# xLSTM attention before two mixture-of-experts layers: padding rows of two loads dropped, q and k turned by one transfer, new planner prices

## The chip, the cores and the metric

The kernel runs on one core of one Trainium2 chip. The metric is device time in microseconds. Three runs of the kernel before took 509.6, 509.74 and 513.57 us; their median is 509.74 us.

## The reference

An attention with exponential gates (B = 2, H = 8 heads, S = 768 tokens, D = 40) feeds two mixture-of-experts layers. Per head and token, with a running maximum m that keeps the exponents in range:

```python
m_new = max(f[t] + m, i[t])
C = exp(f[t] + m - m_new) * C + exp(i[t] - m_new) * outer(v[t], k[t])
n = exp(f[t] + m - m_new) * n + exp(i[t] - m_new) * k[t]
y[t] = sigmoid(o[t]) * (C @ q[t]) / max(|n . q[t]|, 1)
```

The 1536 rows of 320 values then go through a dense layer of four experts (weights 320 x 1024 and 1024 x 320, weighted by the given domain probabilities), and through a routed layer of eight experts, where each row goes to its best expert, up to a capacity of 384 rows each.

## The kernel before

**Attention.** The tokens are cut into 12 units of 128 tokens of one batch (units 0 to 5 are batch 0). `front(u)` loads a unit, makes the decays and computes the scores (S); `back(u)` makes the output rows (B), splits them into 16-bit parts and turns the 128 x 640 block with a transposing transfer (`turn`, line 563, issued at line 565) into the tile `xT[:, u]`, from which the dense experts' first layer reads. `back` also updates the running state C.

Units 0 to 3 (`FP`) are computed in fp32. Their q and k come already transposed from `att_t` (line 849): 128 rows of 1024 words, where each head's 40 rows are padded with zeros to 64, so that a pair of heads fills 128 rows. The scores (line 999) take 64 rows of it, the product with the state (`inter32`, line 1099) all 128.

Units 4 to 11 split q and k into 16-bit parts, three parts of 40 values padded to 128 columns per head: ScalarE (line 911) writes the high part, VectorE (line 917) the remainder, for q first, then for k. After each of the two, SyncE issues a turn of 1024 columns (line 923). The scores (line 1003) need both, the product with the state (line 1089) needs q's only.

For units 4 to 11 the decays' exponents come from one bf16 matmul per half of the heads over 24 rows (`args`, line 959). These rows stand for the time being in the tiles `xT` of units 4 to 11: a load of constants `lr` (line 774, 64 partitions x 8 units x 1280 bytes; of each 32 partitions 24 are used) writes ones and zeros, and then 16 small loads (line 783), three rows each, write the gates' numbers over some of them. They come from `lr_dram`, to which line 771 stored them.

**Experts.** `tile_ops` (line 636) runs first layer (L, line 577), its evacuation by ScalarE and VectorE (lines 596, 598) and second layer (M, line 589) of dense experts 0 and 1, tile by tile, between the steps of the attention. Weights of all experts are loaded as fp32 into two raw buffers, measured (line 465), scaled and split into two 16-bit parts (lines 514, 519). Dense experts 2 and 3, routing and the routed experts follow.

**What sets the order.** Nothing is issued directly. Every step is added to a list with an engine, a price in us and the keys that it reads and writes (`Sched.add`). `urgency` computes the latest start of each step from prices and `LAT`, the time after an engine's step until its result can be used; TensorE's steps follow each other by their place in the written list `SEQ` (line 671). `sch.ahead` moves the latest start of the steps added while it is set: a positive number makes them more urgent, a negative one less. `starts` then fills the engines greedily: among the steps that are ready when an engine is free (or will be within `HOLD`), the most urgent goes next. The program is written in the order of these starts, so each engine and each queue (SyncE issues all these transfers, in one queue) works its steps strictly in that order. Where the plan has a gap on TensorE of over 0.15 us, `gaps` puts dummy matmuls on zeros of about the gap's length (line 365) into it.

Of the kernel before, what the change touches and what calls it, by code (L numbers as in the profile page):

```python
# [63 lines left out]
class Sched:  # L64
# [4 lines left out]
    LAT = {"NONE": 0.0, "PE": 0.2, "ACT": 0.15, "DVE": 0.13, "POOL": 0.1, "DMA": 2.1, "SCAT": 2.0}  # L69
    HOLD = {"PE": 0.024, "ACT": 0.342, "DVE": 0.001, "POOL": 0.15, "DMA": 0.519, "NONE": 0.0}  # L70
# [64 lines left out]
    def starts(self, lst):  # L135
        ops = self.ops
        n = len(ops)
        unit = ["POOL" if op[0] == "SCAT" else op[0] for op in ops]
# [63 lines left out]
def xlstm_moe_kernel(ctx: ExitStack, tc: tile.TileContext, a, cap: int):  # L202
# [110 lines left out]
    RAWKEYS = K("raw", 3) + K("raw2", 3) + K("og", 3) + [("Rp", i, *p) for i in range(3) for p in PARTS]  # L313
# [249 lines left out]
    def turn(dst, src, r, w):  # L563

        add("DMA", 0.62, lambda: nc.sync.dma_start(out=dst, in_=src[:, 0:640], transpose=True), r, w)
# [28 lines left out]
    def evac_ops(ph, kp, hh, hl, kh, kl, extra=()):  # L594
        ex = list(extra)
        act(0.48, lambda: nc.scalar.activation(out=hh, in_=ph, func=AF.Relu), [kp] + ex, [kh])  # L596
# [7 lines left out]
    def l2_ops(k, t, wb, hh, hl, j, keys, at, extra=()):  # L604
        kp = ps_tile("o")
        po = bank[kp]
        for half in range(2):
# [10 lines left out]
            0.15, lambda: nc.gpsimd.tensor_tensor(cf, pw[:, t, k:k + 1], invx[:, t:t + 1], ALU.mult),  # L618
# [17 lines left out]
    def tile_ops(k, t, at, at2):  # L636
# [3 lines left out]
        for g in range(2):  # L640
# [3 lines left out]
                "PE", 1.72,  # L644
# [29 lines left out]
    NFP = len(FP)  # L674
    ARGS, AT_ARGS = 0.75, {1: -0.6, 2: 1.4, 3: 4.5}
# [22 lines left out]
    dma(probs, a["moe_domain_probs"].rearrange("(t p) e -> p t e", p=128), 0.5, [], ["probs"])  # L698
# [63 lines left out]
    for x, v, t, kv, kt in ((3, ig, mc, "ig", "mc"), (0, pc, fg, "pc", "fg")):  # L762
# [11 lines left out]
    dma(  # L774
        xTf.bitcast(I32)[0:64, NFP:], a["lr"].unsqueeze(1).to_broadcast([64, NT - NFP, 320]), 2.0, ["lrd"],
        [("xT", u) for u in range(NFP, NT)],
    )
    for x in range(2):
        for h in range(H):
# [5 lines left out]
                lr_dram[h, NFP:, x].rearrange("u r t -> r u t"), 0.5, ["lrd"] + [("xT", u) for u in range(NFP, NT)], [("LR", h, x)],  # L785
            )
    add(
# [44 lines left out]
    for u in FP[:2]:  # L832
        pool(0.5, lambda u=u: nc.gpsimd.memset(k32p[u % 2], 0.0), [], [("Wh0", u % 2), ("Wh1", u % 2)])

    def front(u):
# [12 lines left out]
        if fp:  # L848
            dma(raw[:, 0:QN0], a["att_t"][u], 1.47, [], [kr] + [("Rp", i3, *p) for p in PARTS])
            dma(raw[:, KN0:OG0], a["att"][b, c][:, HD:3 * HD], 0.97, [], [kr2])  # L850
        else:
            if u - 3 in FP:
                add("NONE", 0.0, lambda: None, [], [kr] + [("Rp", i3, *p) for p in PARTS])
# [24 lines left out]
        if not fp:  # L878
# [25 lines left out]
            for x in range(2):  # L904
# [16 lines left out]
                add(  # L921
                    "DMA", 0.9,
                    lambda x=x: nc.sync.dma_start(
# [144 lines left out]
    def back(u):  # L1068
# [58 lines left out]
        for j in range(2):  # L1127
            if fp:
                add("PE", 0.79, lambda j=j: intra32(j), [("wf", i3, j), kr2], ["x2"], at)
                continue  # L1130
# [766 lines left out]
```

## Time and profile before

| What | Value |
|---|---|
| median of the runs shown | 509.74 us |
| profiled execution | 511.15 us |
| its span, first to last instruction | 509.2 us |
| mean granted TensorE clock | 0.988 |
| busy TensorE / VectorE / ScalarE / GpSimd | 95% / 67% / 61% / 24% of the span |
| dummy matmuls on zeros | 94 |

How to read it: busy time is the time in which an engine worked on an instruction; matmul ends are modelled, and matmuls that follow each other overlap in these numbers. A line L577 is line 577 of the kernel. "PE" is TensorE, "DVE" VectorE, "ACT" ScalarE, "POOL" GpSimd, "SPq" SyncE's queue. A bracket after a row of a timeline gives the time for which the engine stood idle before it, and what ended that. The attention and dense experts 0 and 1 fill the first 235 us. A transfer's row on SyncE is only its issue; when it lands is seen by who waits for it.

### The profile page before, as it was taken

How to read it: one execution, taken by the hardware profiler on the slowest of the kernel's cores; microseconds unless marked ns; L12 is line 12 of the kernel's file. 1: busy time of each engine (PE TensorE's matmuls, PEld its weight loads, DVE VectorE, ACT ScalarE, POOL GpSimd, SP SyncE). 2: the span in 40 equal slices, each digit the busy share in tenths (PEclk: the TensorE clock that was granted, in tenths of full speed). 3: DMA queues.
4: the chain of work that ended last, by engine and by line, in shares of the span. 5: the costliest groups of instructions: out<-in, count | busy, mean ns of one | idle time of the engine just before them, and what ended most of it. 6: DMA issues, size and time to landing. Idle time of an engine off the chain costs nothing.

```text
span 509.2 us, 13776 instructions
## 1 busy us (share of the span) xinstructions
PE 486.1 (95%) x5489; PEld 371.8 (73%) x5489; DVE 341.2 (67%) x988; ACT 311.2 (61%) x648; POOL 123.5 (24%) x239
## 2 busy tenths in 40 slices
PE   8997999999999999999999999899999999999993
PEld 7987887878777988886564647365554798888882
DVE  4697996988968977447779584688969891212120
ACT  3995888566656876667767486998866241322220
POOL 3641244465353500211000000000411220310201
PEclk9998999999999999999999999899999999999997
DMA  6899394533523489734897876655453356999000
GB/s 214 321 258 218 91 261 126 138 77 84 108 52 49 101 270 301 249 97 141 315 318 240 351 248 237 197 160 148 137 145 114 116 165 80 307 257 302 28 24 24
DMA packets 76267, 89.96 MB, mean 177 GB/s; under 512 B 53773, under 2 KB 61604, under 8 KB 76198
## 3 DMA queue, kind: packets, MB, share of 16 engines
q1 hardware_dynamic: 74998, 85.30, 57.9%
q0 software_dynamic: 1200, 3.73, 2.0%
q8 instruction: 45, 0.74, 0.6%
q14 instruction: 24, 0.20, 0.1%
HBM read 56.84 MB, written 21.82 MB: 154 GB/s over the span
## 4 chain that ended last, share of the span: by engine, by line
PE 31%; DVE 22%; DMA 19%; issue 13%; ACT 11%; POOL 2%; SPq 1%; POOLq 0%; another core or an unknown queue 0%; ACTq 0%; DVEq 0%
PE ph L577 11%; PE po L589 11%; DMA raw<-in_moe_w_dram 7%; DVE w L519 5%; ACT junk L465 4%; DMA wsm<-wsm 4%; DVE arena L598 3%; ACT w L514 2%; PE x L577 2%; DMA xT<-arena 2%; PE ph L365 2%; DMA arena<-in_att_dram 1%; DMA arena<-arena 1%; ACT arena L514 1%; ACT arena L596 1%
## 5 line engine op out<-in xcount | busy, mean ns | idle before, releaser
L589 PEld LDWEIGHTS <-arena 128*128 128x128 f16 x1416 | 135.5, 98 | 52.8 <-issue 1.1
L577 PEld LDWEIGHTS <-w 128*128 128x128 f16 x1792 | 99.9, 99 | 7.2 <-issue 5.8
L577 PE MATMUL ph<-xT,w 128*128 128x128 f16 (+2 forms) x1664 | 98.6, 219 | 4.0 <-DMA xT<-arena 3.0
L577 PEld LDWEIGHTS <-arena 128*128 128x128 f16 x960 | 66.8, 98 | 47.6 <-issue 5.4
L589 PE MATMUL po<-w,arena 128*128 128x320 f16 x600 | 87.5, 299 | 0.0
L465 ACT ACTIVATE junk<-raw 128x512 bf16<-128x512 f32 (+1 forms) x108 | 71.5, 662 | 14.8 <-DMA raw<-in_moe_w_dram 12.9
L589 PE MATMUL po<-arena 128*128 128x320 f16 x504 | 72.1, 299 | 0.0
L577 PE MATMUL ph<-xT,arena 128*128 128x512 f16 (+3 forms) x512 | 68.7, 287 | 2.1 <-DVE arena L598 2.1
L598 DVE SCALAR_TENSOR_TENSOR arena<-ph,arena 128x512 f16<-128x512 f32 x80 | 54.5, 684 | 22.2 <-ACT arena L596 21.9
L596 ACT ACTIVATE arena<-ph 128x512 f16<-128x512 f32 x80 | 47.0, 589 | 31.1 <-PE ph L577 29.0
L519 DVE SCALAR_TENSOR_TENSOR w<-raw,wsm,w 128x640 f16<-128x640 f32 (+1 forms) x56 | 57.6, 1056 | 4.2 <-ACT w L514 4.1
L514 ACT ACTIVATE w<-raw,wsm 128x640 f16<-128x640 f32 (+1 forms) x56 | 51.2, 961 | 11.6 <-DVE wsm L396 11.3
L577 PE MATMUL x<-xT,arena 128*128 128x128 f16 (+3 forms) x448 | 53.2, 273 | 0.4 <-issue 0.4
L589 PE MATMUL x<-arena 128*128 128x320 f16 x240 | 34.9, 299 | 0.0
L407 POOL CROSS_LANE_REDUCE wsm<-wsm 128x1 f32<-128x6 f32 (+1 forms) x24 | 7.7, 321 | 106.7 <-ACT junk L465 93.5
L519 DVE SCALAR_TENSOR_TENSOR arena<-raw,wsm,arena 128x640 f16<-128x640 f32 (+1 forms) x28 | 28.9, 1047 | 2.6 <-ACT arena L514 2.6
L514 ACT ACTIVATE arena<-raw,wsm 128x640 f16<-128x640 f32 (+1 forms) x28 | 25.4, 957 | 6.0 <-DVE wsm L396 6.0
L1650 POOL DMA_INDIRECT out_dram<-acc,usm x13 | 12.8, 983 | 53.3 <-ACT acc L1647 45.2
L1064 POOL TENSOR_TENSOR arena<-arena 128x512 f16<-128x512 f32 x16 | 19.6, 1239 | 17.9 <-ACT arena L1060 17.8
L1644 DVE SCALAR_TENSOR_TENSOR arena<-ph,arena 128x512 f16<-128x512 f32 x10 | 6.9, 692 | 24.8 <-ACT arena L1639 24.8
L1644 DVE SCALAR_TENSOR_TENSOR arena<-x,arena 128x512 f16<-128x512 f32 x10 | 6.9, 691 | 24.3 <-ACT arena L1639 24.3
L1338 POOL DMA_INDIRECT disp<-arena x12 | 13.1, 1090 | 39.1 <-DVE arena L1330 11.5
(224 smaller groups left out, 660.3 us busy)
## 6 DMA issues: line engine op xcount, KB each, us to landing
raw<-in_moe_w_dram SPq DMA_DIRECT2D x36, 512.0 KB
raw<-in_moe_w_dram SPq DMA_DIRECT2D x24, 640.0 KB
ws<-w SPq DMA_DIRECT2D x8, 768.0 KB
ws<-w SPq DMA_DIRECT2D x8, 640.0 KB
arena<-in_att_dram SPq DMA_DIRECT2D x8, 492.0 KB
disp<-zero SPq DMA_DIRECT2D x1, 3936.0 KB
arena<-ws SPq DMA_DIRECT2D x4, 768.0 KB
arena<-ws SPq DMA_DIRECT2D x4, 640.0 KB
```

Source lines behind the costliest of these rows:

```text
L365: nc.tensor.matmul(out=bank[name][:, 0:256], lhsT=zero16[:, 0:128], rhs=zero16[:, 0:256], start=True, stop=True)
L465: nc.scalar.activation(out=junk[:, 0:w], in_=raw[:, i * w:(i + 1) * w], func=AF.Abs, accum_out=am[:, i:i + 1])
L514: lambda sl=sl: nc.scalar.activation(out=wh[:, sl], in_=raw[:, sl], func=AF.Copy, scale=sc),
L519: lambda sl=sl: nc.vector.scalar_tensor_tensor(wl[:, sl], raw[:, sl], sc, wh[:, sl], ALU.mult, ALU.subtract),
L577: nc.tensor.matmul(out=out, lhsT=wb[wi][:, c, f * 128:(f + 1) * 128], rhs=rhs(xc), start=(i == 0), stop=(i == LAST))
L589: nc.tensor.matmul(out=po[:, 0:DM], lhsT=hs[:, f, sl], rhs=ws[:, f, :], start=(f == 0 and i == 0), stop=(f == NF - 1 and i == 2),)
L596: act(0.48, lambda: nc.scalar.activation(out=hh, in_=ph, func=AF.Relu), [kp] + ex, [kh])
L598: 0.6, lambda: nc.vector.scalar_tensor_tensor(hl, ph, 0.0, hh, ALU.max, ALU.subtract),
L1064: 1.1, lambda j=j: nc.gpsimd.tensor_tensor(Wl[:, j::2], pb[:, j::2], Wh[:, j::2], ALU.subtract),
L1338: sent[k("done")] = nc.gpsimd.indirect_dma_start(out=disp_t[t], out_offset=bass.IndirectOffsetOnAxis(ap=sli, axis=0), in_=R.bitcast(U32), ...
L1644: nc.vector.scalar_tensor_tensor(hl, ph, 0.0, hh, ALU.max, ALU.subtract)
L1650: nc.gpsimd.indirect_dma_start(out=view_of(), out_offset=bass.IndirectOffsetOnAxis(ap=ix[0:n], axis=0), in_=acc[0:n, y], in_offset=None, b ...
```

## The change

- Transposed q and k of units 0 to 3: `att_t` holds 2 x 40 rows of 1024 words per unit instead of 128. Two loads put them at partitions 0 and 64; the rows between are never loaded. Three memsets on GpSimd write zeros into the q part of the three raw buffers first, and the loads wait for them. The scores take 40 rows instead of 64.
- Exponent constants: two loads of 24 partitions, at partitions 0 and 32, instead of one of 64. These two and the 16 row loads are added with `sch.ahead = -8.0`. The row loads wait for both.
- q and k of units 4 to 11: one turn of 2048 columns after both are split, instead of two of 1024.
- Domain probabilities: laid out on the host so that a partition's 48 words are contiguous.
- The planner has a new kind of step, `TURN`, for turns: it stands in SyncE's queue like other transfers, but its result is taken as usable 3.0 us after it instead of 2.1. A turn of a tile is priced 1.25 us instead of 0.62, that of q and k 1.4 instead of twice 0.9.
- Prices, beside those in the diff: evacuation by ScalarE 0.48 to 0.52; coefficient on GpSimd 0.15 to 0.26; half a first layer of a tile 1.72 to 1.8; remainder of decayed k 0.75 to 0.95 and of the weighted scores 1.1 to 1.3, both on GpSimd; TensorE's `intra32` 0.79 to 0.91, `intra` 0.28 to 0.31, `update32` 0.85 to 0.97, `update` 0.6 to 0.71. `SEQ` is unchanged.

```diff
--- before.py
+++ after.py
-    LAT = {"NONE": 0.0, "PE": 0.2, "ACT": 0.15, "DVE": 0.13, "POOL": 0.1, "DMA": 2.1, "SCAT": 2.0}
-    HOLD = {"PE": 0.024, "ACT": 0.342, "DVE": 0.001, "POOL": 0.15, "DMA": 0.519, "NONE": 0.0}
+    LAT = {"NONE": 0.0, "PE": 0.2, "ACT": 0.15, "DVE": 0.13, "POOL": 0.1, "DMA": 2.1, "SCAT": 2.0, "TURN": 3.0}
+    HOLD = {"PE": 0.024, "ACT": 0.342, "DVE": 0.001, "POOL": 0.15, "DMA": 0.519, "NONE": 0.0, "TURN": 0.519}
...
         n = len(ops)
-        unit = ["POOL" if op[0] == "SCAT" else op[0] for op in ops]
+        unit = [{"SCAT": "POOL", "TURN": "DMA"}.get(op[0], op[0]) for op in ops]
...
     PARTS = [(x, y) for x in range(2) for y in "hlc"]
-    RAWKEYS = K("raw", 3) + K("raw2", 3) + K("og", 3) + [("Rp", i, *p) for i in range(3) for p in PARTS]
+    RAWKEYS = [(("raw", i), j) for i in range(3) for j in range(2)] + K("raw2", 3) + K("og", 3) + [("Rp", i, *p) for i in range(3) for p in PARTS]
...
-        add("DMA", 0.62, lambda: nc.sync.dma_start(out=dst, in_=src[:, 0:640], transpose=True), r, w)
+        add("TURN", 1.25, lambda: nc.sync.dma_start(out=dst, in_=src[:, 0:640], transpose=True), r, w)
...
     NFP = len(FP)
+    LR_AHEAD = -8.0
...
     pool(0.1, lambda: nc.gpsimd.tensor_copy(run, base), ["const"], ["run"])
-    dma(probs, a["moe_domain_probs"].rearrange("(t p) e -> p t e", p=128), 0.5, [], ["probs"])
+    dma(probs, a["moe_domain_probs"], 0.5, [], ["probs"])
...
     xTf = xT.rearrange("p u a b -> p u (a b)")
-    dma(
-        xTf.bitcast(I32)[0:64, NFP:], a["lr"].unsqueeze(1).to_broadcast([64, NT - NFP, 320]), 2.0, ["lrd"],
-        [("xT", u) for u in range(NFP, NT)],
-    )
+    sch.ahead = LR_AHEAD
+    for j in range(2):
+        dma(
+            xTf.bitcast(I32)[32 * j:32 * j + 24, NFP:], a["lr"][j].unsqueeze(1).to_broadcast([24, NT - NFP, 320]), 0.9,
+            ["lrd"], [("xT", u) for u in range(NFP, NT)] if j == 0 else ["lr2"],
+        )
...
                 xTf.bitcast(BF16)[r0:r0 + 3, NFP:, c0:c0 + 128],
-                lr_dram[h, NFP:, x].rearrange("u r t -> r u t"), 0.5, ["lrd"] + [("xT", u) for u in range(NFP, NT)], [("LR", h, x)],
-            )
+                lr_dram[h, NFP:, x].rearrange("u r t -> r u t"), 0.5, ["lrd", "lr2"] + [("xT", u) for u in range(NFP, NT)], [("LR", h, x)],
+            )
+    sch.ahead = 0.0
...
         pool(0.5, lambda u=u: nc.gpsimd.memset(k32p[u % 2], 0.0), [], [("Wh0", u % 2), ("Wh1", u % 2)])
+    for i in range(3):
+        pool(0.5, lambda i=i: nc.gpsimd.memset(rawr[i][:, 0:512], 0.0), [], [("rz", i)])
...
         if fp:
-            dma(raw[:, 0:QN0], a["att_t"][u], 1.47, [], [kr] + [("Rp", i3, *p) for p in PARTS])
+            for j in range(2):
+                dma(
+                    raw[64 * j:64 * j + D, 0:QN0], a["att_t"][u, j], 0.95, [("rz", i3)],
+                    [(kr, j)] + [("Rp", i3, *p) for p in PARTS if p[0] == j],
+                )
             if u - 3 in FP:
-                add("NONE", 0.0, lambda: None, [], [kr] + [("Rp", i3, *p) for p in PARTS])
+                add("NONE", 0.0, lambda: None, [], [(kr, 0), (kr, 1)] + [("Rp", i3, *p) for p in PARTS])
...
                 )
-                add(
-                    "DMA", 0.9,
-                    lambda x=x: nc.sync.dma_start(
-                        out=qkT[:, x], in_=R2[:, x].rearrange("p h e -> p (h e)"), transpose=True
-                    ), [key(y) for y in "hlc"], [("qk", i3, x)],
-                )
+            add(
+                "TURN", 1.4,
+                lambda: nc.sync.dma_start(
+                    out=qkT.rearrange("p x h e -> p (x h) e"), in_=R2.rearrange("p x h e -> p (x h e)"), transpose=True
+                ), [("Rp", i3, x, y) for x in range(2) for y in "hlc"], [("qk", i3, x) for x in range(2)],
+            )
...
             add(
-                "PE", 0.46, args, [("LR", h, x) for h in range(H) for x in range(2)] + [("xT", u)], list(ke),
+                "PE", 0.43, args, [("LR", h, x) for h in range(H) for x in range(2)] + [("xT", u)], list(ke),
...
                 for j in range(2):
-                    r = slice(64 * j, 64 * j + 64)
+                    r = slice(64 * j, 64 * j + D)
...
         add(
-            "PE", *((1.75, scores32, [kr]) if fp else (0.46, scores, [("qk", i3, x) for x in range(2)])),
+            "PE", *((1.1, scores32, [(kr, 0), (kr, 1)]) if fp else (0.46, scores, [("qk", i3, x) for x in range(2)])),
...
-            add("PE", 0.85, inter32, [kr, kC], ["x3"], at)
+            add("PE", 0.95, inter32, [(kr, 0), (kr, 1), kC], ["x3"], at)
...
     att = np.full((B, NC, 128, AW - QN0), TINY, f32)
-    att_t = np.zeros((B, NC, 128, QN0), f32)
+    att_t = np.empty((B, NC, 2, D, QN0), f32)
     for x, t in enumerate((q, k)):
-        y = np.zeros((B, H, 64, S), f32)
-        y[:, :, :D] = t.transpose(0, 1, 3, 2)
-        y = y.reshape(B, NPAIR, 128, NC, 128).transpose(0, 3, 2, 1, 4)
-        att_t[..., 512 * x:512 * (x + 1)] = y.reshape(B, NC, 128, 512)
+        y = t.transpose(0, 1, 3, 2).reshape(B, NPAIR, 2, D, NC, 128).transpose(0, 4, 2, 3, 1, 5)
+        att_t[..., 512 * x:512 * (x + 1)] = y.reshape(B, NC, 2, D, 512)
     r["att"] = att
-    r["att_t"] = np.ascontiguousarray(att_t.reshape(B * NC, 128, QN0)[FP])
+    r["att_t"] = np.ascontiguousarray(att_t.reshape(B * NC, 2, D, QN0)[FP])
     r["f_gate"] = np.ascontiguousarray(inp["f_gate"].transpose(1, 0, 2))
-    lr = np.zeros((2, 32, 5, 128), ml_dtypes.bfloat16)
-    lr[:, 0:12, 0] = 1.0
+    lr = np.zeros((24, 5, 128), ml_dtypes.bfloat16)
+    lr[0:12, 0] = 1.0
     for g in range(NPAIR):
-        lr[:, 12 + 3 * g:15 + 3 * g, 1 + g] = 1.0
-    r["lr"] = lr.reshape(64, 640).view(np.int32)
-    r["moe_domain_probs"] = np.ascontiguousarray(inp["moe_domain_probs"])
+        lr[12 + 3 * g:15 + 3 * g, 1 + g] = 1.0
+    r["lr"] = np.tile(lr.reshape(24, 640).view(np.int32), (2, 1, 1))
+    r["moe_domain_probs"] = np.ascontiguousarray(inp["moe_domain_probs"].reshape(NT, 128, E1).transpose(1, 0, 2))
```

## Rows read from the trace of the kernel before

**Rows 1.** Page, busy us, share of the span, instructions, by engine.
```profile
PE 486.1 (95%) x5489; PEld 371.8 (73%) x5489; DVE 341.2 (67%) x988; ACT 311.2 (61%) x648; POOL 123.5 (24%) x239
```

**Rows 2.** Waits of TensorE, whole span: us in total, times, longest us.
```profile
PE ph L577 <- DMA xT<-arena: 3.0, 2, 2.7
...
PE x L1003 <- DMA arena<-arena: 2.1, 2, 1.1
```

**Rows 3.** Matmul lines, 15 to 46 us: the dummies, count, busy us, mean ns.
```profile
L365 PE MATMUL ph<-zero 128*128 128x256 f16 x36 | 4.9, 273 | 0.0
...
L365 PE MATMUL x<-zero 128*128 128x256 f16 x6 | 1.0, 272 | 0.0
...
L365 PE MATMUL po<-zero 128*128 128x256 f16 x7 | 0.9, 274 | 0.0
```

**Rows 4.** Timeline of TensorE, 0 to 235 us: start, us, line, tiles, wait before.
```profile
10.40 1.16 PE L999 MATMUL x<-arena 64*128 64x128 f32 x16
...
42.06 1.15 PE L365 MATMUL ph<-zero 128*128 128x256 f16 x9
...
45.88 5.36 PE L577 MATMUL ph<-xT,w 128*128 128x128 f16 x64 [2.67 <-DMA xT<-arena]
...
52.70 3.74 PE L577 MATMUL ph<-xT,w 128*128 128x128 f16 x64
...
67.40 0.39 PE L959 MATMUL x<-xT 24*128 24x512 bf16 x2
```

**Rows 5.** Busy time by stretch: length, each engine, granted clock, transfers.
```profile
45.88:51.07 5.19, 5.19 (x64) 5.19 (x64) 1.66 (x5) 1.49 (x3) 0.00 (x0) 0.67 0.97 258
```

**Rows 6.** Timeline of SyncE, 0 to 60 us: start, us, line, transfer.
```profile
3.12 0.43 SPq L371 DMA_DIRECT2D arena<-in_att_t_dram  x1
...
34.60 0.48 SPq L371 DMA_DIRECT2D probs<-in_moe_domain_probs_dram  x1
...
37.92 0.71 SPq L371 DMA_DIRECT2D xT<-in_lr_dram  x1
...
38.74 1.26 SPq L565 DMA_TRANSPOSE xT<-arena  x1
...
45.31 0.63 SPq L371 DMA_DIRECT2D xT<-lr_dram  x2
```

**Rows 7.** Chain of waits, whole span: start, us, what was waited for.
```profile
38.74 7.09 DMA xT<-arena
...
87.71 3.08 DMA arena<-arena
...
140.48 2.57 DMA xT<-arena
...
156.35 4.38 DMA arena<-arena
```

**Rows 8.** Transfer view, GB/s in 40 slices of 10:20, 38.5:46 and 86:91 us.
```profile
GB/s 410 426 426 459 393 410 410 426 453 376 391 388 436 426 447 442 410 398 379 409 415 465 441 442 360 393 213 33 16 0 33 16 17 1 108 133 369 353 0 123
...
GB/s 358 379 357 252 113 226 199 171 185 232 225 239 205 191 171 259 262 223 223 202 224 228 209 132 72 71 46 51 31 42 36 25 19 14 87 408 382 171 376 341
...
GB/s 0 0 0 0 0 0 0 0 0 0 0 0 41 209 211 217 223 209 217 188 197 184 160 84 197 211 223 213 207 195 217 211 191 166 25 0 105 100 5 0
```

**Rows 9.** Busy time by stretch, as in Rows 5.
```profile
50.00:60.00 10.00, 10.00 (x126) 8.67 (x125) 9.37 (x25) 8.66 (x16) 1.73 (x3) 1.00 0.33 99
```

**Rows 10.** Line of the turn of q and k: shortest, median, longest ns.
```profile
L923 SPq DMA_TRANSPOSE arena<-arena x16: 1233/1263/2115, 61.0 to 166.7; - x16
```

**Rows 11.** Timeline of VectorE, 24 to 172 us, columns as in Rows 4.
```profile
49.47 0.69 DVE L598 SCALAR_TENSOR_TENSOR arena<-ph,arena 128x512 f16<-128x512 f32 x1 [3.53 <-ACT arena L596]
...
154.44 0.55 DVE L917 SCALAR_TENSOR_TENSOR arena<-arena,usm 128x320 f16<-128x320 f32 x1
...
155.31 0.54 DVE L917 SCALAR_TENSOR_TENSOR arena<-arena,usm 128x320 f16<-128x320 f32 x1
```

**Rows 12.** Timeline of GpSimd, 0 to 24 us.
```profile
1.54 0.98 POOL L833 MEMSET arena<- 128x512 f32 x2
```

More of the change, by code (lines that the diff above doesn't have):

```diff
@@ L595, in evac_ops @@
         ex = list(extra)
-        act(0.48, lambda: nc.scalar.activation(out=hh, in_=ph, func=AF.Relu), [kp] + ex, [kh])
+        act(0.52, lambda: nc.scalar.activation(out=hh, in_=ph, func=AF.Relu), [kp] + ex, [kh])
         vec(
@@ L617, in l2_ops @@
         pool(
-            0.15, lambda: nc.gpsimd.tensor_tensor(cf, pw[:, t, k:k + 1], invx[:, t:t + 1], ALU.mult),
+            0.26, lambda: nc.gpsimd.tensor_tensor(cf, pw[:, t, k:k + 1], invx[:, t:t + 1], ALU.mult),
             [("pw", k), ("xs", t, "inv")], [("cf", t, k)],
@@ L643, in tile_ops @@
             add(
-                "PE", 1.72,
+                "PE", 1.8,
                 lambda g=g, ph=ph: l1_quad_mm(wb, g, lambda c: xT[:, t, c], ph),
@@ L1040, in front @@
             pool(
-                0.75, lambda: nc.gpsimd.tensor_tensor(kl, k32, kh, ALU.subtract),
+                0.95, lambda: nc.gpsimd.tensor_tensor(kl, k32, kh, ALU.subtract),
                 [("k32", i2), ("kh", i2)], [("kl", i2)],
@@ L1063, in front @@
             pool(
-                1.1, lambda j=j: nc.gpsimd.tensor_tensor(Wl[:, j::2], pb[:, j::2], Wh[:, j::2], ALU.subtract),
+                1.3, lambda j=j: nc.gpsimd.tensor_tensor(Wl[:, j::2], pb[:, j::2], Wh[:, j::2], ALU.subtract),
                 [("wf", i3, j), (f"Wh{j}", i2)], [(f"Wl{j}", i2)],
@@ L1128, in back @@
             if fp:
-                add("PE", 0.79, lambda j=j: intra32(j), [("wf", i3, j), kr2], ["x2"], at)
+                add("PE", 0.91, lambda j=j: intra32(j), [("wf", i3, j), kr2], ["x2"], at)
                 continue
-            add("PE", 0.28, lambda j=j: intra(j), [(f"Wh{j}", i2), (f"Wl{j}", i2), ("vh", i3), ("vl", i3)], ["x2"], at)
+            add("PE", 0.31, lambda j=j: intra(j), [(f"Wh{j}", i2), (f"Wl{j}", i2), ("vh", i3), ("vl", i3)], ["x2"], at)
         kO = ("O", i2)
@@ L1162, in back @@
             if fp:
-                add("PE", 0.85, update32, [("Wh0", i2), ("Wh1", i2), kr2], ["x3"], at)
+                add("PE", 0.97, update32, [("Wh0", i2), ("Wh1", i2), kr2], ["x3"], at)
             else:
-                add("PE", 0.6, update, [("kh", i2), ("kl", i2), ("vh", i3), ("vl", i3)], ["x3"], at)
+                add("PE", 0.71, update, [("kh", i2), ("kl", i2), ("vh", i3), ("vl", i3)], ["x3"], at)
             def c_add():
```

## Prediction

> **What bounds the kernel now.** I read the page's busy shares first: TensorE is busy for 486.1 of 509.2 us [rows 1], so a change can only pay by the little that TensorE still loses: waits, matmuls at the low clock, and the dummy matmuls on zeros that the planner writes into gaps it foresees. Then the waits of TensorE over the whole span: the largest single one on a transfer is 2.7 us for a turned activation tile xT, and the two turns of q and k for which TensorE waits cost 2.1 us together [rows 2]. Then the matmul lines of 15 to 46 us: 49 dummies on zeros, 4.9 + 1.0 + 0.9 = 6.8 us of modelled time [rows 3]. The timeline of TensorE shows the place: dummies from 42.06 us, then 2.67 us of nothing, then 64 matmuls of a first layer in 5.36 us, where the next 64 like them take 3.74 us [rows 4]. [...] So this one late tile costs 2.67 + (5.36 - 3.74) = 4.29 us.
>
> Why is it late? SyncE's timeline has, in this order, the domain probabilities, the load of the exponent constants (640 KB), and the turn of that tile at 38.74 us [rows 6]. The chain of waits gives the turn 7.09 us to land; an undisturbed one takes 2.57 us [rows 7]. The row loads, which write into the constants' tiles and so wait for them, are issued at 45.31 us [rows 6]: the constants took 7.4 us from their issue. The turn stands in the queue behind them. The transfer view of 38.5 to 46 us shows about 210 GB/s from 39.6 to 42.8 us and then, until 44.9 us, 132 falling to 14 GB/s [rows 8]: a tail in which little moves.
>
> **The change part by part.**
>
> The exponent constants: 640 KB become 2 x 240 KB, in two issues, and the planner's less urgent setting for them and the 16 row loads behind them (8 us) lets it place other transfers first. The turn at 38.74 us is such a transfer. If it goes first it lands after 2.57 us, at 41.3 us [rows 6, 7], before TensorE gets there (42.06 us, [rows 4]). The dummies stay, since the planner now thinks a turn slower, not faster. Gain: 4.29 us. Bounds: nothing, if the order of the two stays; 4.29 us plus the dummies of 42.06 us (9 of them, 1.15 us) if these go too, 5.4 us. I take 4.3 us, because the exponents' rows are wanted only by the matmuls of the fifth unit at 67.40 us [rows 4], and VectorE, though 9.37 us busy in the ten from 50 to 60 [rows 9], stands idle for 3.53 us until these very matmuls feed it at 49.47 us [rows 11], so it can follow TensorE forward. What is late next is VectorE, with its weight splits; from 50 us on it has 0.6 us in ten to spare. The 18 issues that move (0.71 us for the old constants, 0.63 us for two row loads, [rows 6]: some 6 us of SyncE) move past the turns of the first tiles and past weight loads; behind the wait for the constants, which they take along, then stand later turns and loads, and there are 22 us from 45.31 to 67.40 us to place them in.
>
> The probabilities: one load of 1536 pieces of 16 bytes becomes one of 128 pieces. It lies ahead of the turn as well; its time is in the 4.29 us and is not counted again.
>
> The turn of q and k: eight units lose one issue on SyncE each (1.26 us, [rows 10]), and SyncE waits for k's parts before it starts. Nothing on TensorE waits for q's half alone before it also needs k's. VectorE writes q's remainder at 154.44 and k's at 155.31 us [rows 11], 0.87 us apart. Before, the second issue followed the first by 1.26 us and landed 3.08 us later [rows 7]: 4.34 us after q was ready. After, the one issue starts at 0.87 us, takes the same 3.08 us, and 1.2 us more for the second 256 KB at the 215 GB/s that such a pair showed [rows 8]: 5.15 us, so 0.8 us later. For two units TensorE already waits, until about 90.8 and 160.7 us [rows 2, 7], so there nothing covers it: 2 x 0.8 = 1.6 us lost. The other six show no wait; their cover is of unknown size and hides it. Behind SyncE's wait for k's parts stand the copies of the running state, as they stood behind the second turn before. Bounds: below, the issue was the limit and both waits vanish, a gain of 2.1 us [rows 2]; above, a turn of double width takes double the issue, 2.1 us (1.26 + 0.87) later in each of the five units from 85 us on (of seven) whose scores follow the first turn within 6 us. I take 0.8, since turns of 640 and of 1024 columns show nearly the same issue (median 1.26 us for 1024, [rows 10]; 1.26 us for the 640 at 38.74 us, [rows 6]), so width hardly shows in it.
>
> The transposed q and k of the four fp32 units: one load of 128 rows becomes two of 40 rows, four more issues of 0.43 us [rows 6], and three memsets on GpSimd that the first loads now wait for. Two like them took 0.98 us from 1.54 us on [rows 12]. SyncE issued the first load at 3.12 us [rows 6]; the scores that use it start at 10.40 us without a wait [rows 4]. Cost: zero, hidden by these 7.3 us; if the cover were gone, 0.5 us of memset and 0.43 us of issue. Behind that wait on SyncE stand the copies of the running maxima and the first weights, which would be late by the same 0.9 us at most. The scores with 40 instead of 64 rows have as many matmuls of as many columns: zero.
>
> The planner's prices (first layer 1.72 to 1.8, splits on GpSimd, a turn 1.25 + 3.0 instead of 0.62 + 2.1, and others) cost nothing by themselves. They move the order on every engine and the number of dummies. No row of before shows the new order: I bound it by half of the 6.8 us of dummies [rows 3], 3.4 us, on either side, and take zero.
>
> **Sum.** -4.3 + 1.6 = -2.7 us. The profiled execution took 511.15 us (span 509.2), 1.4 above the median of the runs shown, 509.74. On its own time it gives 508.4, on the median **507.0 us**.
>
> **The rivals.**
>
> *The whole early stage tightens.* Prices nearer to what the rows show let the planner put VectorE's work for the first units ahead of weight splits, so half of the dummies go (3.4), the late tile (4.3), and, because the planner starts the splits of q and k earlier for its slower turn, the two waits of 2.1 us too: -9.8 us, **499.9 us**. For it: these losses are there [rows 2, 3] and TensorE is the bound everywhere, so they are real time. Against: the order of TensorE's steps is a written list that does not change, and VectorE has little to give [rows 9].
>
> *The load of constants gets no shorter and stays ahead.* It moved at about 210 GB/s, while loads into all 128 partitions in 10 to 20 us mostly ran at 360 to 465 GB/s until 16 us [rows 8], and its long tail is not explained by its bytes. If it stays before the turn and its time does not fall with its rows, the wait stays as it is and only the joint turn's 1.6 us is added: **511.3 us**. [...]
>
> *The joint turn becomes the bound (slower).* If one issue of 2048 columns takes twice 1.26 us, scores of the five later units come 2.1 us later: 10.5 us, less about 1 us of cover in three of them (3), plus the low clock after the two longest waits (1.6 each, as after the wait before 45.88 us, [rows 4]), less the 4.3 us above: +6.4, **516.1 us**. It decides from about 1.5 us of delay a unit: 2 x 1.5 bare and 3 x (1.5 - 1) behind cover make up the 4.3 us. For it: turns already sit on the chain at 87.71 and 156.35 us [rows 7]. Against: the flat issue time.
>
> **How the numbers follow.** Chances: forecast 0.38, early stage tightens 0.27, constants stay ahead 0.21, joint turn 0.14. About 1% (5 us) is what a measurement of this kernel can tell from no change: below 504.6 is faster, above 514.8 slower. The forecast's own range, by the bounds of the new order, is 503.5 to 510.5, and some 0.13 of its 0.38 lies under 504.6; with the second case's 0.27 that is 0.40 faster. Slower is the last case but a little, 0.13. Same: 0.47. The range must leave out no more than 0.2: 0.07 of the second case below 499 and 0.12 of the last above 514. So 499 to 514 us.
>
> **What would show it.** In the profile after: the turn of the second tile issued before the load of constants, landing in about 2.6 us; no wait of a first layer near 43 us and no granted clock of 0.67 behind it; fewer dummies or as many; single turns of q and k whose issue takes near 1.3 us and which land about 4.3 us after it; TensorE's waits for them at two units 0.8 us longer. The forecast is wrong if the turn still lands in 7 us, if the issue of a joint turn takes 2.5 us, if the exponent matmuls of the fifth unit wait for their rows, or if the dummies grow.

## The result and the profile after

The changed kernel took 516.62 us (median of 6 runs, 515.36 to 520.44), the kernel before beside it 512.7 us (6 runs). The ratio is 1.010, 95% interval 1.0064 to 1.0135: about 1% slower, where 507.0 us, 2.7 less than before, was forecast and 514 was the upper end. All ratios leave out the slow executions, those over 1.5% above the fastest of the same kernel, so they can differ a little from the quotient of the medians.

That ratio did not come again: timed later beside another set of runs, the changed kernel took 516.25 us and the kernel before 516.58 us, ratio 0.998 (0.995 to 1.001). Over six comparisons the kernel before had medians of 512.7, 512.0, 517.2, 512.7, 516.6 and 518.7 us. So there are two questions: where the changed kernel loses 5 us against the kernel before at 512 us, and why it loses nothing against it at 517 us. Each run below is therefore given as a ratio to the kernel before in the same comparison.

The profiled execution took 516.04 us (span 514.3, granted clock 0.983), against 511.15 (509.2) before. Page and waits of TensorE, changed kernel; they answer to [rows 1, 2]:

```profile
PE 488.9 (95%) x5497; PEld 375.0 (73%) x5497; DVE 344.5 (67%) x988; ACT 309.5 (60%) x648; POOL 127.4 (25%) x242
```

```profile
PE x L1299 <- DMA arena<-arena: 5.4, 1, 5.4
PE ph L577 <- DVE arena L598: 4.5, 4, 2.5
...
PE x L1013 <- DMA arena<-arena: 1.1, 1, 1.1
...
PE ph L577 <- DMA xT<-arena: 0.4, 1, 0.4
```

The late tile is gone from the list (2.7 to 0.4), and the waits for q and k fell. New at the top is L1299, the router's matmul in the routing stage, a stage of which the prediction speaks nowhere.

SyncE's queue and TensorE's timeline of the changed kernel show the first step as forecast (they answer to [rows 4, 6]):

```profile
40.33 1.22 SPq L565 DMA_TRANSPOSE xT<-arena  x1
...
48.45 0.82 SPq L371 DMA_DIRECT2D xT<-in_lr_dram  x2
...
55.27 1.97 SPq L371 DMA_DIRECT2D xT<-lr_dram  x3
```

```profile
42.10 2.56 PE L365 MATMUL po<-zero 128*128 128x256 f16 x22
45.04 3.75 PE L577 MATMUL ph<-xT,w 128*128 128x128 f16 x64 [0.37 <-DMA xT<-arena]
```

The turn goes 8 us ahead of the constants, and the first layer runs in 3.75 us, where it took 5.36 before, at a granted clock of 0.67 [rows 5]. But by the end of the attention little is left of it. TensorE's first matmuls of the weights' next stage, before and after:

```profile
237.94 0.38 PE L577 MATMUL ph<-xT,arena 128*128 128x512 f16 x1
```

```profile
237.20 0.38 PE L577 MATMUL ph<-xT,arena 128*128 128x512 f16 x1
```

So in this pair of profiles 0.74 us are gained there, and 5.8 us are lost behind it. The 0.74 us are less than the same start moves between executions of one kernel (see the late tile below). SyncE at 400 to 410 us, before (first fence) and after:

```profile
402.67 1.24 SPq L565 DMA_TRANSPOSE arena<-arena  x1
404.30 2.96 SPq L1409 DMA_TRANSPOSE xT<-disp  x2
```

```profile
404.81 1.24 SPq L1419 DMA_TRANSPOSE xT<-disp  x1
...
406.87 1.20 SPq L565 DMA_TRANSPOSE arena<-arena  x1
```

And TensorE, before and after:

```profile
408.04 1.95 PE L577 MATMUL ph<-xT,arena 128*128 128x128 f16 x32
```

```profile
411.89 0.30 PE L1299 MATMUL x<-wg,arena 128*128 128x16 f16 x5 [5.37 <-DMA arena<-arena]
412.05 3.24 PE L577 MATMUL ph<-xT,arena 128*128 128x128 f16 x32
```

L1409 (after: L1419) is an early read of routed rows out of the table `disp`, and must wait until they are scattered. L565 at this place is the turn of the ninth routed tile. Before, the turn stood ahead of the read; after, behind it, and SyncE stood still for 6.1 us at the read (its waits at 398 to 412 us):

```profile
SPq L1419 <- DMA disp<-arena: 6.1, 1, 6.1
```

The turn's data had long been there: VectorE finished the tile's split at 400.97 us, the turn was issued at 406.87. TensorE waited 5.37 us for it and then ran one layer at the low clock (granted clock 0.57 from 412.05 to 415.20 us), 3.24 instead of 1.95 us. That layer ends at 409.99 before and 415.29 after: 5.3 us, the whole difference of the spans (5.1).

### The profile page after: what moved, and what is told of

Read it like the earlier page. It is cut to its first block, busy times and chain, and to the rows that moved or that the text cites. A ratio compares the mean times of both kernels' runs of the same rounds, so it can differ in the third digit from the quotient of the medians.

```text
span 514.3 us, 13768 instructions
## 1 busy us (share of the span) xinstructions
PE 488.9 (95%) x5497; PEld 375.0 (73%) x5497; DVE 344.5 (67%) x988; ACT 309.5 (60%) x648; POOL 127.4 (25%) x242
## 4 chain that ended last, share of the span: by engine, by line
PE 30%; DVE 24%; DMA 18%; issue 12%; ACT 10%; POOL 2%; SPq 1%; POOLq 0%; another core or an unknown queue 0%; ACTq 0%; DVEq 0%
PE ph L577 11%; PE po L589 10%; DMA raw<-in_moe_w_dram 6%; DVE arena L598 4%; DMA wsm<-wsm 4%; DVE w L519 4%; ACT junk L465 3%; ACT w L514 3%; DVE arena L519 2%; DMA arena<-in_att_dram 2%; PE x L577 2%; DMA usm<-disp 2%; DMA xT<-in_lr_dram 1%; PE ph L365 1%; DMA arena<-arena 1%
## 5 line engine op out<-in xcount | busy, mean ns | idle before, releaser
L577 PEld LDWEIGHTS <-w 128*128 128x128 f16 x1792 | 98.1, 98 | 4.7 <-issue 2.7
L577 PE MATMUL ph<-xT,w 128*128 128x128 f16 (+2 forms) x1664 | 96.2, 218 | 2.4 <-DVE arena L598 2.1
L577 PE MATMUL ph<-xT,arena 128*128 128x512 f16 (+3 forms) x512 | 70.2, 292 | 2.5 <-DVE arena L598 2.5
L407 POOL CROSS_LANE_REDUCE wsm<-wsm 128x1 f32<-128x6 f32 (+1 forms) x24 | 8.8, 365 | 108.1 <-ACT junk L465 94.5
L519 DVE SCALAR_TENSOR_TENSOR arena<-raw,wsm,arena 128x640 f16<-128x640 f32 (+1 forms) x28 | 30.5, 1105 | 1.9 <-ACT arena L514 1.8
L1660 POOL DMA_INDIRECT out_dram<-acc,usm x13 | 12.8, 984 | 48.3 <-ACT acc L1657 41.2
L1074 POOL TENSOR_TENSOR arena<-arena 128x512 f16<-128x512 f32 x16 | 20.7, 1313 | 16.3 <-ACT arena L1070 16.2
L1348 POOL DMA_INDIRECT disp<-arena x12 | 14.9, 1245 | 39.4 <-DVE arena L1283 15.7
## 6 DMA issues: line engine op xcount, KB each, us to landing
raw<-in_moe_w_dram SPq DMA_DIRECT2D x36, 512.0 KB
```

The lines of the kernel that those rows point to most:

```text
L407: pool(us, lambda: nc.gpsimd.tensor_reduce(row, x, AX.XYZWC, ALU.max), r, [(key, "row")])
L519: lambda sl=sl: nc.vector.scalar_tensor_tensor(wl[:, sl], raw[:, sl], sc, wh[:, sl], ALU.mult, ALU.subtract),
L577: nc.tensor.matmul(out=out, lhsT=wb[wi][:, c, f * 128:(f + 1) * 128], rhs=rhs(xc), start=(i == 0), stop=(i == LAST))
L1074: 1.3, lambda j=j: nc.gpsimd.tensor_tensor(Wl[:, j::2], pb[:, j::2], Wh[:, j::2], ALU.subtract),
L1348: sent[k("done")] = nc.gpsimd.indirect_dma_start(out=disp_t[t], out_offset=bass.IndirectOffsetOnAxis(ap=sli, axis=0), in_=R.bitcast(U32), ...
L1660: nc.gpsimd.indirect_dma_start(out=view_of(), out_offset=bass.IndirectOffsetOnAxis(ap=ix[0:n], axis=0), in_=acc[0:n, y], in_offset=None, b ...
```

## The experiments

Three theories stood at the start: (1) the planner's new price of a turn reorders SyncE in the routing stage; (2) the loss is the attention's, by the joint turn or the constants; (3) scores over 40 rows lower the granted clock at the start, which was 0.57 in 12 to 20 us of the changed kernel's profile and 1.00 before.

**The routing price taken back, in the changed kernel.**

```diff
-            turn(xg, R, [...], [("xg", t % 2)])
+            turn(xg, R, [...], [("xg", t % 2)], "DMA", 0.62)
```

> The changed kernel, but the turns of the routing stage are priced for the planner as before (0.62 + 2.1 instead of 1.25 + 3.0); no instruction is added or removed, and SyncE has the turn of the last routed tile ahead of the read of the scattered rows again. Theory 1 (the new price lets that read, which waits 6.1 us for its rows, stand in the queue ahead of the turn, and TensorE waits 5.4 us for it): that wait falls to about 1 us and the 3.24 us of the next first layer to about 1.95, so some 5.5 us less than the changed kernel, 508 to 511 us, no difference from the kernel before. Theory 2 (the loss is in the attention stage: the joint turn and the constants): no change, 516 us. Theory 3 (40-row scores lower the clock at the start): no change, 516 us.

Ratio 1.0029 (0.9996 to 1.0062). TensorE:

```profile
384.05 0.30 PE L1299 MATMUL x<-wg,arena 128*128 128x16 f16 x5 [3.58 <-DMA arena<-arena]
...
412.14 0.28 PE L1299 MATMUL x<-wg,arena 128*128 128x16 f16 x5 [0.62 <-DMA arena<-arena]
```

The last wait went from 5.37 to 0.62 us, as theory 1 said, but an earlier routing turn is now 3.58 us late (in the kernel before, 1.2): it is issued at 381.34 us, behind a transfer of the weights' scales for which SyncE waited 6.9 us. So 0.7% came back, not all.

**The routing price alone, in the kernel before.**

```diff
-            turn(xg, R, [...], [("xg", t % 2)])
+            turn(xg, R, [...], [("xg", t % 2)], "TURN", 1.25)
```

> The kernel before, with only the planner's price of the routing stage's turns raised to the new one (1.25 + 3.0). Theory 1: the read of the scattered rows moves ahead of the last turn on SyncE, TensorE waits some 5 us there, and the time is 5 to 6 us above the kernel before, with no other part of the change present. Theories 2 and 3: a price costs nothing, within 1 us of the kernel before.

Ratio 1.009 (1.0056 to 1.0123): with as many instructions on every engine as before, only in another order, nearly the whole loss. The wait is there:

```profile
PE x L1289 <- DMA arena<-arena: 4.9, 1, 4.9
```

Theory 1 holds against a kernel before at 512 us; theories 2 and 3 said that a price costs nothing.

**Scores over 64 rows in the changed kernel, and with the old routing price.**

```diff
-                    r = slice(64 * j, 64 * j + D)
+                    r = slice(64 * j, 64 * j + 64)
```

The memsets are widened with it, so that the padding rows are zeros.

> The changed kernel, but the scores of the fp32 units run over 64 rows as before (the 24 padding rows are zeros, set by wider memsets); the order of every engine is the changed kernel's. Theory 3 (matmuls over 40 rows in place of 64 are what the granted clock of 0.50 from 12 to 18.6 us comes from): granted clock 1.0 there, the 16 scores of weights at 15 us take 1.95 instead of 3.67 us, about 2.5 us less in the early stage, so near 513.5 us. Theories 1 and 2: the same clock of 0.50 at 12 to 18.6 us and 516 us.

> The changed kernel with the old price of the routing turns and with scores over 64 rows. Theories 1 and 3 together: the two gains add, 5.5 + 2.5 us less than the changed kernel, about 508 us, some 3 to 4 us less than the kernel before, since up to the routing stage the changed kernel was 1.7 us ahead of it. Theory 2: 516 us.

Ratios 1.0047 (1.0012 to 1.0082) and 1.0044 (1.0008 to 1.008). Both profiles have clock 1.00 in 12 to 20 us, and the first fell by 0.5%, as theory 3 has it; but the old routing price, worth 0.7% above, gave nothing more in the second. Inconclusive, so the 40 rows were put alone into the kernel before:

> The kernel before, with only the scores of the four fp32 units over 40 of the 64 rows of each head (the other 24 are zeros in the input); every engine's order and every transfer is that of the kernel before. Theory 3 (40-row scores at the start bring the granted clock down at 12 to 19 us): mean granted clock over the runs about 0.006 lower than the kernel before, clock about 0.6 in 12 to 20 us of the profile, 1.5 to 3 us slower. Rival (the low clock at the start comes by chance in any of these kernels, as the kernel before with the routing price had it with 64 rows): same mean clock, within 1 us of the kernel before.

Ratio 1.0013 (0.998 to 1.0047), mean clock of the runs 0.9867 against 0.9872: no cost that can be measured, and theory 3 falls. Its profile has a clock of 0.79 in 12 to 20 us, but two later profiles show that this does not come from the 40 rows. The kernel before, unchanged and with 64 rows, in the first fence; the changed kernel with its 40 rows, timed again, in the second (TensorE busy, granted clock, share of the transfers, GB/s):

```profile
12.00:20.00 8.00, 8.00 (x48) 0.63 0.87 309
```

```profile
12.00:20.00 8.00, 8.00 (x73) 1.00 0.61 196
```

The low clock at the start comes in some executions of either kernel.

**Is it the order, or the price?** The changed kernel with all prices, and an edge in the plan that keeps early reads behind the ninth tile's turn:

```diff
-            turn(xg, R, [...], [("xg", t % 2)])
+            turn(xg, R, [...], [("xg", t % 2)] + (["turn8"] if t == 8 else []))
...
-        add("DMA", 0.62, load, [("nS", i)] + [...], [...])
+        add("DMA", 0.62, load, [("nS", i), "turn8"] + [...], [...])
```

> The changed kernel with all its prices, but the early reads of the scattered rows may not be placed ahead of the turn of the ninth routed tile (an edge in the plan). The planner writes 19 more dummies in the routing stage, 2.4 us by 0.13 us each. Theory 1 (the loss of the routing stage is that order on SyncE, not the prices as such): TensorE's 5.4 us wait for the last turn and the 1.3 us of low clock behind it go, and the wait of 3.6 us for the turn of the sixth tile, which came with the old prices, does not appear; 4 to 6.5 us less than the changed kernel, 509 to 512 us. Rival (the routing stage is late for another reason, and the wait only shows where it ends): another wait of about 5 us takes its place, 515 to 517 us.

Ratio 1.0035 (1.0004 to 1.0067). TensorE:

```profile
406.20 0.28 PE L1299 MATMUL x<-wg,arena 128*128 128x16 f16 x5 [1.06 <-DMA arena<-arena]
406.34 0.92 PE L365 MATMUL ph<-zero 128*128 128x256 f16 x7
...
409.94 1.95 PE L577 MATMUL ph<-xT,arena 128*128 128x128 f16 x32 [0.93 <-DMA xT<-disp]
```

The wait for the turn fell to 1.06 us; the read of the scattered rows is late next, behind 19 dummies. The order was the cause of the long wait. As I read the trace, a TensorE that comes to this stage early meets the scatter's own time there.

**Which part of the change moved the late tile?** Two runs on the kernel before: the less urgent setting of the constants alone (`sch.ahead = -8.0` around their load and the row loads), and the price of the activation turns alone.

> The kernel before, with only the planner's less urgent setting (8 us) for the load of the exponent constants and its 16 row loads; the load keeps its 64 rows. If the gain of 4.3 us of my sum comes from the order (the turn of the second tile goes ahead of the constants), this alone gives it: no wait of 2.7 us near 43 us, no granted clock of 0.67 behind it, and the group stage starts 2 to 4 us earlier. If it comes from the fewer rows, the constants still hold up a turn for some 7 us and nothing is gained.

> The kernel before, with only the planner's price of the activation turns raised (1.25 + 3.0); constants of 64 rows and their urgent setting stay, the routing turns keep the old price. In the planned order the turn of the second tile then stands ahead of the load of the constants, which neither the less urgent setting nor the fewer rows brought about. If the gain of 4.3 us of my sum is that order, this alone gives it: the turn lands in about 2.6 us, no wait of 2.7 us near 43 us, the group stage starts 2 to 4 us earlier than in the kernel before, 2 to 4 us faster. Rival (the late turn is hidden by what is late next, VectorE's splits): the group stage starts within 1 us, no gain.

The setting alone: ratio 1.0001 (0.9967 to 1.0035). SyncE and TensorE:

```profile
37.85 0.71 SPq L371 DMA_DIRECT2D xT<-in_lr_dram  x1
38.68 1.89 SPq L565 DMA_TRANSPOSE xT<-arena  x1
```

```profile
45.73 5.36 PE L577 MATMUL ph<-xT,w 128*128 128x128 f16 x64 [2.77 <-DMA xT<-arena]
```

Nothing moved: constants first, the turn late. The price alone: ratio 1.0028 (0.9997 to 1.0059).

```profile
38.90 1.22 SPq L565 DMA_TRANSPOSE xT<-arena  x1
...
40.80 1.09 SPq L371 DMA_DIRECT2D xT<-in_lr_dram  x1
```

```profile
43.44 3.74 PE L577 MATMUL ph<-xT,w 128*128 128x128 f16 x64
...
74.90 5.37 PE L577 MATMUL ph<-xT,w 128*128 128x128 f16 x64 [2.04 <-DMA xT<-arena]
...
239.34 0.59 PE L577 MATMUL ph<-xT,arena 128*128 128x512 f16 x2
```

The turn goes first, and that first layer ends 4.06 us earlier (47.18 against 51.24 in [rows 4]). So the gain is the price's, not the constants'. Then another tile comes 2.04 us late at 74.90, again with a slow layer behind it, and the next stage starts at 239.34, 1.4 us later than before: in this execution all was given back.

> The same, and the constants in 24 rows and less urgent as in the changed kernel. If fewer rows are worth something by themselves: the row loads start earlier than with 64 rows and the exponent matmuls of the fifth unit wait less, up to 1 us faster than the run with the price alone. Rival (the rows make no difference once the turn is ahead): the same time within 1 us.

With the constants in 24 rows as well: 0.9981 (0.9955 to 1.0007), and again 0.9978 (0.9946 to 1.001). No wait at 75 us here; the row loads start at 46.92 us, where they start at 47.45 with the price alone. In the first comparison that is 0.0047, or 2.4 us, below the price alone; the two intervals still overlap.

> The kernel before, with the new price for all turns of 640 columns and the edge that keeps the early reads behind the ninth tile's turn (19 more dummies). If both lessons hold (the price gains early, the order on SyncE in the routing stage takes it back): no wait over 1.5 us for a routing turn, 2 to 4 us faster than the kernel before; without the edge the routing price alone was 4.6 us slower. Rival (the 19 dummies, 2.4 us, eat it): within 1 us of the kernel before.

Both turn prices with the edge, in the kernel before: 1.0058 (1.0028 to 1.0088), a miss. In its profile the stage after the attention starts 2.5 us early, and TensorE spends that on the dummies of the routing stage and a wait of 0.64 us for the scattered rows. But that profile is of the shortest of its 12 executions (510.73 us, median 515.13), so where the median loses is not shown.

**The joint turn.** Alone in the kernel before; then taken back in the changed kernel with the edge; then added to the price and the constants.

> The kernel before, with only the joint turn of q and k (one transfer of 2048 columns, priced 1.4 + 3.0 for the planner). My sum says 0.8 us later at each of the two units where TensorE already waited: 1.6 us slower, 513 to 514 us. Rival (issue of double width): an issue near 2 us as in the changed kernel, but hidden: TensorE's waits for turns of q and k in sum no more than the 2.1 us of before, within 1 us of it.

> The changed kernel with the edge for the early reads, and q and k of a unit turned by two transfers of 1024 columns as before. My sum says the joint turn costs 0.8 us at each exposed unit: TensorE's waits for q and k and behind them are 1 to 2 us less than with the joint turn and the edge (ratio 1.0035 to the kernel before there, so 1.000 to 1.002 here). Rival (hidden): the same ratio and the same waits within 0.5 us.

> The kernel before with the activation turns' price, the constants in 24 rows and the joint turn of q and k; routing turns at the old price, no edge. If the joint turn is hidden (the changed kernel waits 1.3 us for q and k where the kernel before waits 2.1): TensorE's waits for q and k 1 to 2 us less than with two turns, the time 0 to 1.5 us less than without the joint turn, ratio 0.995 to 0.998 to the kernel before. By my sum (0.8 us at each exposed unit): 1.6 us more, ratio 1.000 to 1.002.

TensorE's waits for q and k, at the line of the scores: 2.1 us before and none listed with the joint turn alone; 3.0 with two turns in the changed kernel with the edge, 0.6 with the joint turn there; 1.1 with two turns beside 0.5 with the joint turn, on the kernel of price and constants. In each pair, one profile each, the joint turn has the shorter waits. The times do not follow them. Alone it took 1.0037 (1.0008 to 1.0066), 1.9 us more, while its waits for activation turns grew from 3.0 to 4.4 us. With two turns and the edge the ratio is 1.0074 (1.0036 to 1.0112), against 1.0035 with the joint turn in another comparison. Added to price and constants it is 0.9971 (0.9937 to 1.0004) beside 0.9978 without, no difference.

**The two levels of the kernel before.** The changed kernel, and the edge, again on one chip:

> The changed kernel itself, timed again, beside the runs of this call on one chip. If the routing stage's order on SyncE is most of the loss, the ratio to the kernel before is again near 1.010 and at least 0.004 above that of the run with the edge on the same chip; if the first ratio was mostly low clock by chance, it is nearer to 1.004. In the trace: TensorE's wait of about 5 us for the last routing turn comes again whatever the clock did earlier; the granted clock at 12 to 19 us may be 0.5 or 1.0.

> The changed kernel with the edge for the early reads, again, beside the changed kernel on one chip. Theory 1: 0.004 to 0.007 below the changed kernel's ratio, some 2 to 3.5 us. Rival (the wait of 5.4 us would be filled by the wait for the scattered rows anyway): within 0.002 of it.

Ratios 0.9981 (0.9951 to 1.001) and 1.0023 (0.9988 to 1.0057): the rival won. The wait is there in the changed kernel (5.01 us, the layer behind it 3.59 us), and yet nothing is lost against the kernel before at 516.6 us. This trace also shows where the early gain goes (SyncE's load, then VectorE, then TensorE, then TensorE's stretch with the clock):

```profile
48.48 0.71 SPq L371 DMA_DIRECT2D wgf<-in_moe_w_gate_dram  x1
```

```profile
58.94 0.18 DVE L1245 TENSOR_REDUCE gsm<-wgf 128x1 f32<-128x24 f32 x1 [2.98 <-DMA wgf<-in_moe_w_gate_dram]
```

```profile
61.01 1.92 PE L1170 MATMUL x<-arena 128*128 128x82 f32 x8 [3.59 <-DVE arena L1116]
```

```profile
60.00:70.00 10.00, 8.99 (x83) 0.66 0.48 105
```

> The kernel before itself, with its trace on this chip. If the 4 us between its levels (512 us in two comparisons, 517 in two) are the gaps put down to issue among the 32-column matmuls at 437 to 446 us: at the level of 517 its trace shows 2 us or more of them, at the level of 512 under 1 us.

> The kernel before with the routing turns' price alone, again, beside the kernel before itself. Theory (TensorE's wait of 5 us in the routing stage and the gaps of issue behind it replace each other): no gaps of issue at 437 to 446 us; where the kernel before is at 517 us the two are within 0.004 of each other, where it is at 512 us this one is again 0.007 to 0.011 slower. Rival (the gaps come with the chip and have nothing to do with the wait): gaps here too, and 0.009 slower at either level.

Medians 518.51 and 518.68 us; the kernel before beside them took 518.65. Ratios 1.0004 (0.9978 to 1.0031) and 0.9986 (0.9952 to 1.0021). TensorE of the kernel before, then of the one with the routing price:

```profile
438.90 0.24 PE L577 MATMUL ph<-xT,w 128*128 128x32 f16 x3 [0.43 <-issue]
439.64 0.31 PE L577 MATMUL ph<-xT,w 128*128 128x32 f16 x6 [0.50 <-issue]
440.37 0.28 PE L577 MATMUL ph<-xT,w 128*128 128x32 f16 x5 [0.42 <-issue]
...
442.78 4.27 PE L589 MATMUL x<-arena 128*128 128x320 f16 x24
```

```profile
412.64 0.30 PE L1289 MATMUL x<-wg,arena 128*128 128x16 f16 x5 [5.29 <-DMA arena<-arena]
...
442.79 0.95 PE L577 MATMUL ph<-xT,arena 128*128 128x32 f16 x32
```

Between its 32-column matmuls the kernel before stands still five times, 2.4 us in all, in which it waits for nothing that the profile shows ("issue"), and the second layer behind them takes 4.27 us, where the profile at 509.2 us has 3.42 at a granted clock of 1.00:

```profile
436.06 3.42 PE L589 MATMUL x<-arena 128*128 128x320 f16 x24
```

Laid beside that profile, this stretch costs 4.1 us. The kernel of price and constants was profiled at both levels, on one chip: there the same stretch takes 5.80 us at the level of 512 and 10.43 at 517, and these 4.6 us are nearly the whole difference of its spans (509.7 and 514.6). The kernel with the 5.29 us wait has none of these gaps. All five profiles with the long routing wait have at most 0.2 us of them, in both kinds of comparison; where the kernel before was at 517 to 519 us, all eight profiles without that wait have 2.1 to 2.8 us of them; where it was at 512, none has over 0.44 us. So against the kernel before at 517 us the wait takes the place of the gaps. Shown is that they replace each other; why the gaps come in some comparisons only, and how the wait keeps them away, stays open. It is not the chip alone: one chip had the kernel before at 512.7, 516.6 and 518.7 us.

## Why the prediction was wrong

**The step that failed** is "The planner's prices ... cost nothing by themselves ... I ... take zero". The price of the routing turns, alone, costs 0.9% against the kernel before at 512 us (and nothing that can be told against it at 519). My bound for it, 3.4 us of dummies, came from the early stage; but a price acts wherever the planner places a step of that kind. What it cost was a wait of SyncE (6.1 us at the read), which now stood in the queue in front of the turn. I had listed what is queued behind SyncE's wait for k's parts, and never asked it of the turns' other user.

**The late tile, -4.3 us:** right in place and size (4.06 us at the end of that layer with the price alone), wrong in its cause. I credited it to the constants' less urgent setting and used the turn's price ("the planner now thinks a turn slower, not faster") only to say that the dummies stay. The setting alone moved nothing, the price did, since the planner must start a step earlier whose result it expects later. And it does not stay: "it can follow TensorE forward" failed. The plan pulls the load of the router's weights `wgf` from 76.45 us to between 48.3 and 51.3 in eight profiles, behind the constants. In the two profiles of the changed kernel VectorE's 102 steps around L1245 (32.13 to 71.83 and 29.85 to 74.01 us) come in the same order, and in the later one VectorE stands 2.98 us at L1245 and TensorE 3.59 behind it, with a granted clock of 0.66 from 60 to 70 us. That the load's place is the cause is read from the trace, not tested by a run. The wait also differs between executions. In those eight profiles VectorE's wait for the load is 2.98, 2.60, 1.97, 1.46, 0.41 and 0.20 us in six and missing in two, the changed kernel's first among them, and what decides that stays open. So no gain at the end of the attention is shown: the next stage starts at 236.59, 237.20, 239.64, 239.77 and 241.66 us in the five profiles of the changed kernel with its own order there (with the edge or the old routing price or neither), and at 236.65, 237.94, 238.97 and 239.37 in the four of the kernel before (with the new routing price or without).

**The joint turn, +1.6 us:** wrong in its mechanism. Its landing was right: issued at 87.32, its scores start at 91.71, 4.4 us later, where 4.3 was forecast. Its issue was not flat, 1.6 to 3.0 us with a median of 1.91:

```profile
L933 SPq DMA_TRANSPOSE arena<-arena x8: 1610/1906/3012, 61.9 to 164.6; - x8
```

```profile
87.32 1.93 SPq L933 DMA_TRANSPOSE arena<-arena  x1
```

```profile
91.71 0.62 PE L1013 MATMUL x<-arena 120*128 120x128 f16 x8 [1.09 <-DMA arena<-arena]
```

But the planner, told 1.4 + 3.0, starts the splits of q and k earlier, the very effect that I gave to the first rival alone: with the joint turn alone VectorE's remainder of q starts 0.3 to 3.4 us earlier in all eight units. The waits, which should have grown by 1.6 us, fell from 2.1 to 1.3 us. That the joint turn alone cost 1.9 us (0.4 to 3.4) is near my number by luck, since no wait for q and k is in that profile.

**The 40 rows and the memsets, zero:** the rows held within 0.5%; the memsets were not run alone, but the first scores start at 10.17 us without a wait. **Dummies:** "fewer or as many" failed, 102 instead of 94. **The constants:** their load was no shorter in the changed kernel, 7.69 us in the chain of waits; what sets its time no run shows. In the kernel before with price and constants the row loads start 5.06 us after it (46.92 after 41.86), with the price alone and 64 rows 6.65 us (47.45 after 40.80). TensorE's waits list none for the exponents' matmuls; but the 7.69 us lie on the chain, and VectorE waited 0.75 us at 62 us for the transfer that SyncE issued behind them.

**The rivals.** The slower end was put on the joint turn (516.1 us); the number came close by luck, the mechanism did not: no such waits appeared. The constants did not stay ahead, and the early stage did not tighten. The wait that decided had no rival at all.

In sum, on the two profiled executions: -0.7 up to 238 us, another -0.7 to 396 us (a routing turn that was 1.2 us late before is in time), +6.7 in the layers around the last routing turn, -0.2 behind them: +5.1.

## What to carry to other kernels

A planner's price is an edit of every place that uses it: before calling it free, list the steps of that kind over the whole program, and for each ask what may now stand in front of it in its queue and what that one waits for. A gain in one stage counts only where the next in-order list can start earlier too; in the traces here VectorE's list or the scatter took the gain back. And when a kernel's own time moves by 1% between comparisons, look at its trace in both before explaining the ratio.

## What the runs showed of the hardware

TensorE's granted clock was 0.57 to 0.64 from 12 to 20 us in five of 20 profiles, of the unchanged kernel too (0.63), 0.79 in a sixth and 1.00 in the other 14. In the changed kernel's first profile it was 0.50 from 12 to 18 us. TensorE was busy for all 8.00 us from 12 to 20 us in those six; in the two of them whose start is listed, the changed kernel's first and the unchanged kernel's later one, it had no idle gap from 9 us on either. In the unchanged kernel the same matmuls up to the dummies of 16 us took 8.53 instead of 5.29 us. These profiles show a fall without a pause, and no run here shows what set it off.

Gaps, most of them of 0.4 to 0.5 us, in which TensorE waits for nothing shown, among 32-column matmuls, were new to me as well: the same kernel on the same chip has none in one profile and 2.2 us of them in another. So was a wait of 5 us (5.01 in the changed kernel timed again, ratio 0.9981) that costs nothing that can be told where such gaps would else come.
